# FFN1 of the first two tile pairs: two weight blocks side by side instead of two token tiles, and w1's last rows partly copied on chip

## The chip, the cores and the metric

The kernel runs on one NeuronCore of a Trainium2 chip. The metric is the device time of one execution in microseconds. Engines are named as in the profile: PE is TensorE (PEld its weight loads), DVE is VectorE, ACT is ScalarE, POOL is GpSimd, SP is the queue that issues most DMAs.

## The reference

`x` is 2048 tokens of 448 features, all in bf16. A layer norm feeds two branches whose outputs are added to `x`: a linear attention with 16 heads of 28 features, and a feed-forward network with 1792 hidden features.

```python
xn = _layernorm(x, axis=-1)
return x + _A_ref(xn, A_wqkv, A_w_phi, A_wo) + _B_ref(xn, B_w1, B_w2)

def _B_ref(x, w1, w2):
    h = jnp.einsum("bsd,df->bsf", x, w1)     # FFN1: 448 -> 1792
    h = _silu(h)
    return jnp.einsum("bsf,fd->bsd", h, w2)  # FFN2
# _A_ref: q, k, v = x @ wqkv; phi = [softmax(q w_phi), softmax(-q w_phi)] (k alike);
#         o = phi_q (phi_k^T v) / (phi_q . sum phi_k + 1e-6); o @ wo
```

## The kernel before

The 2048 tokens are 16 tiles of 128, and tiles go in pairs 0 to 7. For each pair the layer norm is taken token by token (`ln_stats`, `ln_rstd`, `ln_norm`), and the normalized rows are turned on TensorE and evicted to `xnT` (`ln_tr`), which has features on partitions. 448 features are seven blocks of 64: `xnT[:, 0:3]` has the first 384 features of the pair's first tile, `xnT[:, 4:7]` those of the second, and block 3 has the last 64 features of the first tile in its upper partitions (UP, 0 to 63) and of the second in its lower ones (LO, 64 to 127).

All matmuls use half of the array's rows: two with 64 rows each, one on UP and one on LO, run side by side and write different PSUM banks (`mms`, L443, whose instructions carry L446). In `contract` (L474) the two halves work on the two tiles of a pair with the same weight block. A first pass takes four steps (UP rows for the first tile, LO rows for the second), a second pass the other halves in three; between the passes stands a wait of PE for itself (`syncs`), since both passes add into the same banks. For this the last 64 rows of each weight (block `KF`) must lie in both halves, so `load_tail` (L548) loads them twice.

FFN1 is `ffn1_chunk` (L672): units of 512 columns in two banks, then one silu on ACT over both (1024 elements per partition). With one pair (`npair` 1) a unit has four feature blocks of 128 and the matmuls move 128 columns; with two pairs it has two blocks and they move 256. Pairs 0 and 1 do feature blocks 0 to 7 one pair at a time, in four units, and blocks 8 to 13 together, in three.

The layer norm of pairs 0 and 1 (`ln_pair_sqrt`, L623) takes the square root on ACT (L630) and the reciprocal on DVE; later pairs take a power on POOL (L599). `ln_pair_first` places matmuls on `ident` (`warm`, L528) around the first transposes. ACT changes from its sqrt table to silu after the square roots of pair 1.

The SP queue issues, in program order: x tile 0, w1 columns 0 to 511 (rows 0 to 383), x tiles 2-3, w1 columns 512 to 1023 with its two tails, x tiles 4-5, w1 columns 1024 to 1791 with its two tails, x tiles 6-7. ACT issues x tile 1 and the first two tails. The loads in `paced` (x tiles 8-11, wqk, x tiles 12-15, wv) wait for the layer norms of pairs 1 to 4; those of w2 and wo wait for exponentials of k.

The order on each engine is not written by hand: a planner (`schedule`, `_Prog`) places every operation by program order, priority and assumed durations, under its data dependences and under order-only ones (`odeps`) within an engine. The instructions then wait on semaphores where the planner saw a dependence.

After FFN1 of pairs 2 to 5 come the folding of `w_phi` into wqk, then k, v, q and the attention state with FFN1 of the rest in between, and then for each pair the second FFN layer and the output projection. In that last phase `q_divide` (L915) makes the attention output of a pair: DVE does the division (L926 to L939), and five additions (`oadd`, L961) bring it into `o_sum`, the tile `xn_sb`. They run on POOL, except that for the last pair all but the first run on DVE. `o_transpose` turns the result on PE into a bank that `out_store` (L990, DVE) must have emptied.

Of the kernel before, what the change touches and what calls it, by code (L numbers as in the profile page):

```python
# [8 lines left out]
ACTF = mybir.ActivationFunctionType  # L9
# [323 lines left out]
def bass_parallel_sum__linear_kernel_hedgehog__dense_activation_silu__prompt_kernel(  # L333
# [12 lines left out]
    KF = 3  # L346
# [8 lines left out]
    with es:  # L355
# [82 lines left out]
        def mm(dst, lhsT, rhs, start, stop, name, dur=None):  # L438
            return P.op("pe", dur or d_mm(_cols(rhs)),
                        lambda e: e.matmul(dst, lhsT, rhs, start=start, stop=stop, skip_group_check=True),  # L440
                        reads=[lhsT, rhs], writes=[dst], table=128, name=name)
# [83 lines left out]
        qpad = wqk_sb[:, :, 0, :, 56:64]  # L525
        P.op("pool", d_pool(256, 0.9), lambda e: e.memset(qpad, 0.0), writes=[qpad], name="qpad")
        P.op("pool", d_pool(256, 0.9), lambda e: e.memset(wraw[:, :, 2 * D:], 0.0), writes=[wraw[:, :, 2 * D:]], name="wpad")
        def warm(n, cols=128):  # L528
            rhs = ident[:, None, :].broadcast_to([128, cols // 128, 128])
            dst = banks[3][:, 0:cols].rearrange("p (a c) -> p a c", c=128)  # L530
            for i in range(n):
                mm(dst, ident[:], rhs, True, True, "warm", cols * 0.836)
            return P.ops[-1]

        def load(dst, src, nbytes, name, eng="sp"):
            return P.dma(lambda e: e.dma_start(out=dst, in_=src), nbytes, writes=[dst], name=name, eng=eng)  # L536
# [4 lines left out]
        def load_x(t0, t1, eng="sp"):  # L541
            return load(x_sb[:, t0:t1, :], xt[:, t0:t1, :], (t1 - t0) * 128 * D * 2, f"x{t0}", eng)

        def load_k(dst, src, c0, c1, name, eng="sp", o=0):
            return load(dst[:, 0:KF, c0 - o:c1 - o], src[0:384, c0:c1].rearrange("(k p) f -> p k f", p=128),
                        384 * (c1 - c0) * 2, name, eng)

        def load_tail(dst, src, c0, c1, name, eng="sp", eng2="sp", o=0):  # L548
            return [load(dst[r, KF, c0 - o:c1 - o], src[384:448, c0:c1], 64 * (c1 - c0) * 2, name, e)
                    for r, e in ((UP, eng), (LO, eng2))]  # L550

        x1_op = load_x(1, 2, "act")
        pre_op.odeps.add(x1_op.id)
        w1t = load_tail(w1_sb, B_w1, 0, 512, "w1at", "act", "act")
        for o in w1t:
            o.odeps.add(pre_op.id)
        load_x(0, 1)
        load_k(w1_sb, B_w1, 0, 512, "w1a")
        load_x(2, 4)
        for c0, c1 in ((512, 1024), (1024, FF)):  # L560
            load_k(w1_sb, B_w1, c0, c1, "w1b")
            load_tail(w1_sb, B_w1, c0, c1, "w1bt")
            if c0 == 512:
                load_x(4, 6)
        load_x(6, 8)
        first_loads = len(P.ops)
        paced = []
# [52 lines left out]
            else:  # L620
                copy_dve(dst, src, "xnT_ev", d_dve(128 * n, 2))

        def ln_pair_sqrt(p):  # L623

            for t in (2 * p, 2 * p + 1):
                k = len(P.ops)
                ln_stats(t)
                if t % 2:
                    P.ops[k].odeps.add(k - 2)
                P.op("act", 220, lambda e, t=t: e.activation(std[:, t:t + 1], mv[:, t, 1:2], ACTF.Sqrt, bias=epsc[:]),  # L630
                     reads=[mv[:, t, 1:2], epsc[:]], writes=[std[:, t:t + 1]], table="sqrt", name="std")
            for t in (2 * p, 2 * p + 1):
                P.op("dve", 150, lambda e, t=t: e.reciprocal(rstd[:, t:t + 1], std[:, t:t + 1]),
                     reads=[std[:, t:t + 1]], writes=[rstd[:, t:t + 1]], name="rstd")
                ln_norm(p, t)

        def ln_pair_first(bk):
            ln_pair_sqrt(0)
            prev = None
            for n, js, eng in ((19, [0, 1, 2], "act"), (2, [3, 4, 5, 6], "dve")):  # L640
                k = len(P.ops)
                o = warm(n, 256)
                if prev:
                    P.ops[k].odeps.add(prev)
                k = len(P.ops)
                ln_tr(0, js, bk if eng == "act" else bk - 2, eng)
                P.ops[k].odeps.add(o.id)
                prev = P.ops[-1].id - 1
            ev = P.ops[-1]
            k = len(P.ops)  # L650
            o = warm(5, 256)
            P.ops[k].odeps.add(prev)
            return ev, o

        def ln_pair(p, one_by_one=False):
            t0, t1 = 2 * p, 2 * p + 1
            for t in (t0, t1):
                ln_stats(t)
                if one_by_one:
                    ln_rstd(t, t + 1)  # L660
            if not one_by_one:
                ln_rstd(t0, t1 + 1)
            ln_norm(p, t0)
            ln_norm(p, t1)
            ln_tr(p, [0, 1, 2, 3, 4, 5, 6], 6, "dve")

        silus = []
        exps = set()
# [3 lines left out]
        def ffn1_chunk(p0, npair, f0, fend, units=(0, 2, 4)):  # L672
            n = npair * 128
            F = 512 // n
            while f0 < fend:
                f1 = min(fend, f0 + F)
                b0 = units[unit_no[0] % len(units)]
                unit_no[0] += 1
                jobs = []
                for ft in range(f0, f1):  # L680
                    jobs.append((lambda r, b: xnT[r, b, p0:p0 + npair, :].rearrange("p a c -> p (a c)"),
                                 lambda r, k, ft=ft: w1_sb[r, k, ft * 128:ft * 128 + 128],
                                 [banks[b0 + par][:, (ft - f0) * n:(ft - f0) * n + n] for par in range(2)],
                                 ft == f0, True))
                units_done.append(contract(jobs, n, True, True, "ffn1_mm"))
                w = f1 - f0
                src = psum[:, b0 * 512:(b0 + 2) * 512].rearrange("p (r c) -> p r c", r=2)[:, :, 0:w * n]
                if w == 1:
                    dst = hT[:, f0, :, p0:p0 + npair, :].rearrange("p r a c -> p r (a c)")
                else:  # L690
                    src = src.rearrange("p r (f c) -> p r f c", f=w)
                    dst = hT[:, f0:f1, :, p0:p0 + npair, :].rearrange("p f r a c -> p r f (a c)")
                o = act(dst, src, ACTF.Silu, "silu", table="silu")
                if exps:
                    o.odeps.update(exps)
                silus.append(o)
                f0 = f1

        def exp_act(dst, src, scale, name):
            o = act(dst, src, ACTF.Exp, name, table="exp", scale=scale)  # L700
# [38 lines left out]
                else:  # L739
                    copy_dve(dst, src, "fold_ev", d_dve(n))  # L740

        last0, warm0 = ln_pair_first(6)
        k = len(P.ops)
        ln_pair_sqrt(1)
        ln_tr(1, [0, 1, 2], 6, "act")
        ln_tr(1, [3, 4, 5, 6], 4, "dve")
        sqrt_last = [o.id for o in P.ops if o.name == "std"][-1]
        for o in P.ops[k:]:
            if o.eng == "dve":
                o.odeps.add(last0.id)  # L750
        last1 = P.ops[-1].id
        k = len(P.ops)
        ffn1_chunk(0, 1, 0, 4, (0, 2))
        P.ops[k].odeps.add(warm0.id)
        silus[0].odeps.add(sqrt_last)
        ffn1_chunk(0, 1, 4, 8, (0, 2))
        ffn1_chunk(1, 1, 0, 4, (4,))
        ffn1_chunk(1, 1, 4, 8, (0,))
        k = len(P.ops)
        ln_pair(2)  # L760
        for o in P.ops[k:]:
            if o.eng == "dve":
                o.odeps.add(last1)
        ln_pair(3)
        ffn1_chunk(0, 2, 8, FT, (2, 4, 0))
        ln_pair(4)
        ffn1_chunk(2, 2, 0, 4)
        ln_pair(5)
        for i in range(3):
            ffn1_chunk(2, 2, 4 + 2 * i, 6 + 2 * i)  # L770
            fold_tr(3 * i)
        ffn1_chunk(2, 2, 10, FT)
        P.cur_prio = 2
        late_constants()
        P.cur_prio = 0
        for kt in range(4):
            ffn1_chunk(4, 2, 2 * kt, 2 + 2 * kt)
            fold(kt)
        ln_pair(6)
        ffn1_chunk(4, 2, 8, 12, (0, 4))  # L780
        ln_pair(7)

# [132 lines left out]
        def q_divide(p):  # L915
# [40 lines left out]
            segs = [seg(0, 0, 0, 448), seg(1, 448, 384, 392), seg(1, 456, 392, 448), seg(1, 512, 0, 336), seg(1, 848, 336, 384)]  # L956
            oadd_last[p] = []
            for i, (dst, a0, a1) in enumerate(segs):
                eng = "dve" if i and p == NPAIR - 1 else "pool"
                o = P.op(eng, d_pool(_cols(dst), 2.26) if eng == "pool" else d_dve(_cols(dst)),  # L960
                         lambda e, dst=dst, a0=a0, a1=a1: e.tensor_tensor(dst, a0, a1, ALU.add),  # L961
                         reads=[a0, a1], writes=[dst], name="oadd")
                oadd_last[p].append(o.id)
# [89 lines left out]
        for a, c in zip(chain, chain[1:]):  # L1053
            for o in c:
                o.odeps.add(a[-1].id)
        evs = [o.id for o in P.ops if o.name == "xnT_ev"]
        for o, d in zip(paced, evs[3:7]):
            o.deps.add(d)
        eks = [o.id for o in P.ops if o.name == "exp_k"]
        for o, d in zip(w2_loads + [wo_load], eks[0::2]):  # L1060
            o.deps.add(d)
# [111 lines left out]
```

## Time and profile before

| | |
|---|---|
| time, median of 3 executions | 158.67 us (158.19 to 159.33) |
| the profiled execution, its own time | 159.27 us |
| its span, first to last instruction | 157.5 us |
| PE busy | 151.2 us (96%), 2655 matmuls |
| DVE, ACT, POOL busy | 100.9, 75.1, 52.9 us |
| granted TensorE clock | 1.0 |
| FFN1 of all pairs (`psum<-xnT,w_sb`) | 896 matmuls, 48.9 us |

A row of the profile gives the line of the kernel, the engine, the operation, the output and inputs by name, and how often it ran; then its busy time, the mean of one, and the idle time before it with what ended it. A row of the timeline begins with the start and the length in microseconds, and in brackets has the idle time before it and its releaser; equal neighbours are merged (x38). The chain of waits is followed back from the last instruction; "issue" in it is time in which the engine waited for nothing that the profile shows. A matmul's end is modelled, so neighbours overlap in the rows.

### The profile page before, as it was taken

The page shows a single profiled execution, that of the slowest core. Times are in us where ns is not written, and L with a number is a line of the kernel's source. Part 1 is how long each engine was busy: PE and PEld are TensorE (multiplying, and loading weights), DVE is VectorE, ACT ScalarE, POOL GpSimd, SP SyncE. Part 2 cuts the span into 40 slices and gives each one's busy share as a digit, 9 for nine tenths or more (in the row PEclk, how much of TensorE's full clock was granted, in tenths as well). Part 3 has the DMA queues.
Part 4 walks back from the last instruction along what each step waited for, and adds up shares of the span by engine and source line. Part 5 has one row for each costly group of instructions (what it writes and reads, how often), then busy time and mean ns, then how long its engine had stood idle before and what let it go on. Part 6 is the DMA issues. An engine that isn't in the chain of part 4 may idle for free.

```text
span 157.5 us, 5805 instructions
## 1 busy us (share of the span) xinstructions
PE 151.2 (96%) x2655; PEld 100.0 (64%) x2655; DVE 100.9 (64%) x180; ACT 75.1 (48%) x88; POOL 52.9 (34%) x74
## 2 busy tenths in 40 slices
PE   6996999999999999999999999999999999999992
PEld 4685888888864445445468887545555655554782
DVE  1886796863236889496796487794755748396203
ACT  3376557458789886996869755120210202022000
POOL 7001111120100777839577023633516060602000
PEclk9999999999999999999999999999999999999999
DMA  4983367000004332040000000001011010101012
GB/s 144 303 262 116 69 163 220 7 0 4 4 0 116 110 113 78 0 121 0 0 4 2 4 4 0 4 4 58 19 43 58 4 58 4 62 2 58 4 58 62
DMA packets 8309, 9.24 MB, mean 59 GB/s; under 512 B 1436, under 2 KB 8028, under 8 KB 8284
## 3 DMA queue, kind: packets, MB, share of 16 engines
q1 hardware_dynamic: 7980, 8.62, 18.2%
q8 instruction: 21, 0.34, 0.9%
q10 hardware_dynamic: 304, 0.25, 0.5%
q14 instruction: 4, 0.03, 0.1%
HBM read 7.02 MB, written 1.84 MB: 56 GB/s over the span
## 4 chain that ended last, share of the span: by engine, by line
PE 88%; DVE 4%; DMA 3%; issue 2%; SPq 2%; DVEq 0%
PE psum L446 85%; DMA w_sb<-in_B_w_dram 3%; PE psum L459 3%; SPq L536 2%; DVE wraw L939 1%; DVE out_sb L990 1%; DVE xn_sb L961 0%; DVE R L926 0%; DVE rden L933 0%; DVE Gq L934 0%; DVE Dd L928 0%; PE psum L877 0%; DVE den L930 0%; DVEq L1113 0%
## 5 line engine op out<-in xcount | busy, mean ns | idle before, releaser
L446 PE MATMUL psum<-xnT,w_sb 64*128 64x256 bf16 (+1 forms) x896 | 48.9, 256 | 1.7 <-issue 1.3
L446 PE MATMUL psum<-w_sb,hT 64*128 64x448 bf16 (+2 forms) x504 | 46.6, 328 | 0.0
L446 PEld LDWEIGHTS psum<-xnT,w_sb 64*128 64x128 bf16 x896 | 37.2, 94 | 7.4 <-issue 1.5
L465 ACT ACTIVATE hT<-psum 128x1024 bf16<-128x1024 f32 x28 | 28.1, 1023 | 15.7 <-PE psum L446 14.3
L446 PEld LDWEIGHTS psum<-w_sb,hT 64*128 64x128 bf16 x504 | 23.1, 94 | 16.1 <-ACT oT L465 0.4
L961 POOL TENSOR_TENSOR xn_sb<-wraw 128x448 bf16<-128x448 f32 (+4 forms) x36 | 19.7, 580 | 36.9 <-DVE wraw L939 36.9
L465 ACT ACTIVATE oT<-psum 128x896 bf16<-128x896 bf16 x8 | 7.3, 917 | 40.8 <-PE psum L459 40.8
L810 POOL TENSOR_TENSOR scr<-scr,Rk 128x1792 bf16<-128x1792 bf16 x6 | 19.3, 3211 | 17.6 <-ACT scr L465 12.7
L465 ACT ACTIVATE EqT<-psum 128x1024 bf16<-128x1024 f32 x16 | 15.5, 1021 | 6.0 <-PE psum L446 6.0
L939 DVE TENSOR_TENSOR wraw<-psum,Gq 128x1792 f32<-128x1792 f32 (+1 forms) x9 | 16.4, 1817 | 0.7
L446 PE MATMUL psum<-xnT,wqk_sb 64*128 64x512 bf16 x112 | 14.8, 378 | 0.0
L990 DVE TENSOR_TENSOR out_sb<-psum,x_sb 128x896 bf16<-128x896 f32 (+2 forms) x9 | 8.8, 980 | 8.6 <-PE psum L446 8.5
L926 DVE RECIPROCAL R<-psum 128x64 f32<-128x64 f32 (+1 forms) x9 | 4.6, 512 | 15.0 <-PE psum L446 15.0
L446 PE MATMUL psum<-wv_sb,xnT 64*128 64x448 bf16 x112 | 14.0, 349 | 0.0
L446 PE MATMUL psum<-wo_sb,oT 64*128 64x448 bf16 (+2 forms) x126 | 13.6, 328 | 0.0
L446 PE MATMUL psum<-wqk_sb,xnT 64*128 64x448 bf16 x112 | 13.2, 349 | 0.0
L590 DVE BATCH_NORM_STATS2 st<-x_sb 128x6 f32<-128x448 bf16 x16 | 9.8, 613 | 4.0 <-DMA x_sb<-in_A_x_dram 4.0
L599 POOL TENSOR_TENSOR rstd<-ve,neghalf 128x2 f32<-128x2 f32 x6 | 4.2, 694 | 24.3 <-DVE ve L598 24.3
L802 DVE TENSOR_REDUCE Sk<-scr 128x64 f32<-128x1792 bf16 x6 | 12.1, 2010 | 0.0
L469 DVE CAST scr<-psum 128x896 bf16<-128x896 f32 x6 | 6.5, 1083 | 8.5 <-PE psum L446 8.5
L465 ACT ACTIVATE scr<-psum 128x896 bf16<-128x896 f32 x12 | 10.4, 915 | 0.7
L446 PEld LDWEIGHTS psum<-wo_sb,oT 64*128 64x128 bf16 x126 | 6.1, 94 | 4.6 <-ACT oT L465 0.2
(64 smaller groups left out, 135.4 us busy)
## 6 DMA issues: line engine op xcount, KB each, us to landing
out_dram<-out_sb SPq DMA_DIRECT2D x7, 224.0 KB, 1.9
w_sb<-in_B_w_dram SPq DMA_DIRECT2D x3, 448.0 KB, 3.4
x_sb<-in_A_x_dram SPq DMA_DIRECT2D x2, 448.0 KB, 4.6
w_sb<-in_B_w_dram SPq DMA_DIRECT2D x2, 384.0 KB, 4.8
x_sb<-in_A_x_dram SPq DMA_DIRECT2D x3, 224.0 KB, 4.9
wraw<-in_A_wqkv_dram SPq DMA_DIRECT2D x1, 672.0 KB, 4.3
w_sb<-in_B_w_dram SPq DMA_DIRECT2D x1, 576.0 KB, 6.6
wv_sb<-in_A_wqkv_dram SPq DMA_DIRECT2D x1, 336.0 KB, 4.8
```

The costliest lines, as they stand in the source:

```text
L446: r = e.matmul(dst, lhsT, rhs, start=start, stop=stop, skip_group_check=True)
L459: out = e.transpose(dst, src, ident[r, 64:128] if r == LO else ident[r, 0:64])
L465: return P.op("act", d_act(_cols(src)), lambda e: e.activation(dst, src, func, scale=scale), reads=[src], writes=[dst], table=table, name= ...
L469: return P.op("dve", dur, lambda e: e.tensor_copy(dst, src), reads=[src], writes=[dst], name=name)
L590: P.op("dve", 600, lambda e: e.bn_stats(st6[:, t, :], x_sb[:, t, :]), reads=[x_sb[:, t, :]], writes=[st6[:, t, :]], name="bnst")
L599: P.op("pool", 580, lambda e: e.tensor_tensor(r2, v2, nh, ALU.pow), reads=[v2, nh], writes=[r2], name="rstd")
L802: P.op("dve", d_dve(896 * n), lambda e, S4=S4, E4=E4: e.tensor_reduce(S4, E4, AXL.X, ALU.add), reads=[E4], writes=[S3], name="Sk")
L810: lambda e, E5=E5, R5=R5: e.tensor_tensor(E5, E5, R5, ALU.mult),
L926: P.op("dve", d_rec(32 * n), lambda e, R3=R3, U=U: e.reciprocal(R3, U[:, :, :, DH + 1]), reads=[U[:, :, :, DH + 1]], writes=[r2], name="R2")
L939: P.op("dve", d_dve(896 * n), lambda e, dsto=dsto, U=U, G3=G3, n=n: e.tensor_tensor(dsto, U[:, :, :, 0:DH], G3[:, :, :, None].broadcast_to ...
L961: lambda e, dst=dst, a0=a0, a1=a1: e.tensor_tensor(dst, a0, a1, ALU.add),
L990: P.op("dve", d_dve(2 * (c1 - c0)), lambda e: e.tensor_tensor(dst, ob, xs, ALU.add), reads=[ob, xs], writes=[dst], name="out_ev")
```

## The change

FFN1 of pairs 0 and 1 gets a function of its own, `ffn1_single`. The two row halves now hold two different weight blocks, and both move the same 256 columns, the two tiles of one pair; the halves change places in the second pass. The last 64 features of both tiles must therefore lie in both halves: the layer norm writes them twice (`lnz_norm`), and they go through PE into a separate tile `xnTt`. The normalized rows and `xnTt` lie in a part of `EqT` that is unused until later. The first unit of a pair does its first pass tile by tile, with 128 columns. Each pair has four units (blocks 0-3, 4-7, 8-11, 12-13).

Evictions of the transposes go by tile: for pair 0 tile 0 on ACT and tile 1 on DVE, for pair 1 tile 2 on DVE and tile 3 on ACT. Pair 1 takes its power on POOL, tile by tile, in place of the square root. The matmuls on `ident` go in row halves. Later users of block 3 of `xnT` for these pairs are served by four DMA copies (`lnz_rest`).

On the SP queue w1's columns 512 to 1023 now stand ahead of x tiles 2-3, and columns 1024 to 1791 ahead of x tiles 4-5. The tails of columns 512 to 1791 are loaded once, into LO, and ACT copies them into UP. The loads in `paced` wait for the last evictions of pairs 1 to 4. Two smaller edits: units of pairs 2 and 3 take the banks in the order 4, 0, 2, and of the last pair's five additions only one (336 columns) stays on DVE.

```diff
-        load_x(2, 4)
-        for c0, c1 in ((512, 1024), (1024, FF)):
-            load_k(w1_sb, B_w1, c0, c1, "w1b")
-            load_tail(w1_sb, B_w1, c0, c1, "w1bt")
-            if c0 == 512:
-                load_x(4, 6)
+        load_k(w1_sb, B_w1, 512, 1024, "w1b")
+        load(w1_sb[LO, KF, 512:FF], B_w1[384:448, 512:FF], 64 * (FF - 512) * 2, "w1t")
+        load_x(2, 4)
+        load_k(w1_sb, B_w1, 1024, FF, "w1c")
+        load_x(4, 6)
         load_x(6, 8)
...
+        def lnz_rest(p):
+            for t, r in enumerate((UP, LO)):
+                a, b = xnT[r, 3, p, :], xnTt[r, p, t, :]
+                o = P.dma(lambda e, a=a, b=b: e.dma_start(out=a, in_=b), 64 * 256, reads=[b], writes=[a], name="xnTt")
...
+            order = [warm(19), lnz_tr(0, 0), warm(3), lnz_tr(0, 1), warm(1)]
+            lnz_ev(0, 0, ("act", "act"))
+            ev = lnz_ev(0, 1, ("dve", "dve"))
...
+        def lnz_second(p):
+            k = len(P.ops)
+            for t in range(2):
+                ln_stats(2 * p + t)
+                ln_rstd(2 * p + t, 2 * p + t + 1)
+            for t in range(2):
+                lnz_norm(p, t)
+                lnz_tr(p, t)
+                ev = lnz_ev(p, t, (("dve", "dve"), ("act", "act"))[t])
...
+        def ffn1_single(p, f0, f1, b0, by_tile=False):
+            h = (f1 - f0) // 2
...
+            for q, t0, t1 in (((0, 0, 1), (0, 1, 2), (1, 0, 2)) if by_tile else ((0, 0, 2), (1, 0, 2))):
+                rr = (UP, LO) if q == 0 else (LO, UP)
+                for k in range(KF + 1 - q):
+                    for i in range(h):
+                        parts = []
+                        for j in range(2):
+                            r, ft = rr[j], f0 + j * h + i
+                            xx = xnTt[r, p, t0:t1, :] if k == KF else xnT[r, k + 4 * t0:k + 4 * t1 - 3:4, p, :]
...
+        a, b = w1_sb[UP, KF, 512:FF], w1_sb[LO, KF, 512:FF]
+        act(a, b, ACTF.Identity, "w1t")
...
+        banks_ = iter((0, 2, 4, 0, 2, 4, 0, 2))
+        for p in range(2):
+            for f0 in range(0, FT, 4):
...
+                done = ffn1_single(p, f0, min(FT, f0 + 4), next(banks_), f0 == 0)
...
-                eng = "dve" if i and p == NPAIR - 1 else "pool"
+                eng = "dve" if i == 3 and p == NPAIR - 1 else "pool"
...
-        for o, d in zip(paced, evs[3:7]):
-            o.deps.add(d)
+        for o, d in zip(paced, evp):
+            o.deps.add(d.id)
```

## The prediction

> **What bounds the kernel now.** I read the page's totals and chain first, then the chain in order of time, then the timeline of each engine where the chain leaves TensorE.
>
> ```profile
> PE 151.2 (96%) x2655; PEld 100.0 (64%) x2655; DVE 100.9 (64%) x180; ACT 75.1 (48%) x88; POOL 52.9 (34%) x74
> q8 instruction: 21, 0.34, 0.9%
> PE 88%; DVE 4%; DMA 3%; issue 2%; SPq 2%; DVEq 0%
> ```
>
> TensorE is busy for 96% and carries 88% of the chain. A change pays only if it gives TensorE less work, an earlier start, or fewer waits. The chain of waits from the start shows where it waits:
>
> ```profile
> 3.52 4.87 DMA w_sb<-in_B_w_dram
> 13.00 1.31 issue
> 14.31 1.21 PE psum L446 x35
> ```
>
> ```profile
> 7.06 1.28 PE L446 MATMUL psum<-xnT,w_sb 64*128 64x128 bf16 x38
> 8.52 0.73 PE L446 MATMUL psum<-xnT,w_sb 64*128 64x128 bf16 x20 [0.18 <-DMA w_sb<-in_B_w_dram]
> 15.49 0.84 PE L446 MATMUL psum<-xnT,w_sb 64*128 64x128 bf16 x24
> 16.17 0.28 PE L459 MATMUL psum<-ident,xn_sb 64*128 64x64 bf16 x8
> 16.29 2.59 PE L446 MATMUL psum<-xnT,w_sb 64*128 64x256 bf16 x44
> 18.71 0.25 PE L459 MATMUL psum<-ident,xn_sb 64*128 64x64 bf16 x6
> ```
>
> This is TensorE's timeline. A matmul of one row half runs beside that of the other, so I count pairs: 12 pairs of 128 columns take 16.17-15.49 = 0.68, **57 ns** each; 22 pairs of 256 columns take 18.71-16.29 = 2.42, **110 ns** each. A 128-column matmul is drawn 216 ns long (the group's mean), so a gap in the chain understates the wait by 216-57 = 0.16 us. FFN1's waits before are then: 0.34 for w1 at 8.4, 0.21 twice where a second pass waits for its first (10.36 and 12.16), 1.31+0.16 = 1.47 at 13.00, and some 0.1 later: **2.3 us**. What ends the 1.47 is no semaphore: the last matmul of the third unit has none. It is TensorE's matmul 222 (26 warm, 28 transposes, 168 FFN1), its instruction 444 with weight loads. The instruction queue's 21 packets serve 5310 instructions, 253 each, and the trace has the first of them only at 11.85 us, while w1 and x still load. I read the wait as an instruction block that came late.
>
> ```profile
> 9.94 1.28 ACT L465 ACT_TABLE_LOAD   x1
> 12.32 0.71 POOL L599 TENSOR_TENSOR rstd<-ve,neghalf 128x2 f32<-128x2 f32 x1 [8.47 <-DVE ve L598]
> 12.47 0.63 DVE L590 BATCH_NORM_STATS2 st<-x_sb 128x6 f32<-128x448 bf16 x1 [0.23 <-DMA x_sb<-in_A_x_dram]
> ```
>
> From these I take prices, and from two of the rows landing times: w1's second tail (1472 KB issued by then) lands at 3.52+4.87 = 8.38, x6-8 (2688 KB) at 12.44: 300 KB/us between.
>
> ```profile
> 141.34 1.79 DVE L961 TENSOR_TENSOR xn_sb<-wraw 128x8 bf16<-128x8 f32 x4
> 141.39 1.13 POOL L961 TENSOR_TENSOR xn_sb<-wraw 128x448 bf16<-128x448 f32 x1 [4.54 <-DVE wraw L939]
> 143.05 1.08 DVE L990 TENSOR_TENSOR out_sb<-psum,x_sb 128x896 bf16<-128x896 f32 x1
> 144.28 0.38 PE L459 MATMUL psum<-ident,xn_sb 64*128 64x64 bf16 x14 [0.22 <-DVE out_sb L990]
> ```
>
> Near the end TensorE waits once more: VectorE does four of the last pair's adds (L961) before the output add (L990) whose bank the last transposes need.
>
> **The change, part by part.**
>
> *TensorE's work.* Before: 112 pairs of 128 and 42 of 256, 6.4+4.6 = 11.0 us. After, by the built order: 32 of 128 and 82 of 256, 1.8+9.0 = 10.8. The two new transpose pairs cost 0.06. **Gain 0.1**: the wider moving operand buys almost nothing, since 128 columns already run at half the price of 256.
>
> *Start.* FFN1 began at 7.06, when VectorE had evicted tile 1. The by-tile unit needs tile 0 alone, evicted by ScalarE in 5.85 to 6.34; with 0.09 to hand over it starts at 6.43. **Gain 0.63**. Tile 1 is evicted by about 7.0, when tile 0's eight pairs are just through (6.9). The dropped w1 tails (320 KB) against one of 160 KB are in the landing times below. Warm matmuls go in halves, the same columns.
>
> *New waits.* I walk the built order. On SP x2-4 moves behind w1b and w1t, x4-6 behind w1c. Landings at 300 KB/us around the 8.38 row: w1t (1280 KB) 7.74, x2-4 (now 1504 KB, behind w1b and w1t) 8.49, w1c (2080 KB) 10.4.
> - The first unit and the second up to its tail rows are 16 pairs of 128 and 12 of 256: 2.2 us, to 8.66. The tail of the upper half waits for ScalarE's copy: 1280 elements, between 0.92 us for 896 and 1.02 for 1024 elements continued, 1.23: 7.79 to 9.02. Wait 0.43.
> - 2 pairs, a pass wait of 0.22, 3 pairs: 9.86. Then tile 2's transposes stand in line. Its input lands at 8.49; stats 0.62, aggregate 0.18, ve 0.17 and hand-overs make 9.58, GpSimd's rstd 0.70 makes 10.35, the normalize 0.37 ends at 10.76. Wait 0.97.
> - At 11.3 a unit needs bank 0, so silu 0: 9.02 + table 1.28 + silu 1.02 = 11.3. No wait, but no slack. w1c is there.
> - Tile 3's normalize (second rstd on GpSimd): 0.2. A pass wait 0.22. Tile 3's eviction behind silu 1 on ScalarE: 0.17. Later some 0.1.
>
> Together **2.3, as much as before**: the 1.47 and the w1 wait go, and waits for the copy, tile 2 and tile 3 take their place. The 1.47 goes because matmul 222 now lies at the end of the unit on bank 4, near 14.5 to 15.3, while the block before it is passed near 7.5, not 9: 7 us for a fetch that took 5.3.
>
> [...]
>
> *x8-12* is issued after tile 3's last eviction, 13.4, where before it was issued by 10.9. The page's 448 KB row lands after 4.6: 18.0, and tile 8's stats, wanted at 17.0, would hold TensorE 0.6. The 112 KB row (2.6) plus 336 KB at 300 gives 3.7 and no wait. The queue is idle then: I take 0.2.
>
> *Nothing on the path:* the four tail copies in lnz_rest stand on SP behind wv and ahead of w2, near 25 to 28 us, where SP waits for the first exponentials until 48.27; uncovered they are four issues of some 0.5. The other bank order and GpSimd's two narrow rstd fall on idle time, apart from those counted.
>
> *The tail.* VectorE keeps one add of four (0.50 for 336 columns), so the output add starts near 141.85, ends at 142.9. GpSimd's four adds end 1.80 after 141.39, or 0.45 later if VectorE's add holds it up: 143.2 to 143.6. TensorE is ready at about 143.8. **Gain 0.4** (0.22 plus the 349-94 ns by which a 448-column matmul is drawn too long, less the usual turn).
>
> ```profile
> L961 DVE TENSOR_TENSOR xn_sb<-wraw 128x56 bf16<-128x56 f32 x1 | 1.2, 1165 | 0.0
> L961 POOL TENSOR_TENSOR xn_sb<-wraw 128x56 bf16<-128x56 f32 x7 | 2.1, 302 | 0.0
> ```
>
> VectorE's 56 columns took 1165 ns while GpSimd's 448-column add ran. [...]
>
> **Sum.** 0.63 + 0.1 + 0.0 - 0.2 + 0.4 = **0.9 us** less. The profiled execution took 159.27 (span 157.5 and 1.77 around it), 0.6 over the median of 158.67, so 158.4 by its own time and **157.8** against the median. From the bounds (x8-12 0 to 0.6, tail 0 to 0.5, landings 0.3 either way) its own range is 157.2 to 158.6.
>
> **Rivals.**
> 1. *The loads come earlier than by the straight line.* If w1t lands at 7.0 and x2-4 at 7.6 (before, x2-4 was third and its stats ran at 6.89), the copy costs nothing, silu 0 ends at 10.6 and the unit at 11.3 starts at 10.4, held by w1c: 0.9 less, **156.9**. For it: w1's 160 KB are gone. Against: 300 KB/us was sustained, and the queue is as full.
> 2. *Slower: ScalarE's queue hangs on the w1 copy.* Behind it stand the table load, silus 0 and 1 and tile 3's eviction. From a landing of about 8.1 each us later costs one; the gain is gone at 9.0, and 10.8 gives 157.8+2.7 = **160.5**. For it: the page's 96 KB tails took 6.2 us to land. Against: those stood behind 576 KB.
> 3. *The 1.47 wait stays*, at its place in the stream or another: **159.3**. For it: no release is recorded. Against: the longer time to fetch.
>
> **How the numbers follow.** Forecast 0.42, rival 1 0.31, rival 2 0.14, rival 3 0.13. A measurement of this kernel tells about 1% from no change: faster than 157.08 is rival 1, 0.31; slower than 160.26 is rival 2, 0.14; the rest 0.55. The range, 156.5 to 159.7, takes in rivals 1 and 3 and leaves out most of rival 2.
>
> **What would show it.** First FFN1 matmul near 6.4; a 1.2 us copy on ScalarE ending near 9.0; TensorE idle near 9.9 for about 1 us with VectorE's normalize as releaser; no "issue" wait near 13 to 15; no wait for out_sb before the last transposes. An idle stretch of over 1.5 us before 20 us, or a first silu after 11, would make the prediction wrong.

## The result: 0.9% slower, and the profile after

The changed kernel takes 159.6 us (median of 18 executions, 158.81 to 161.48), the kernel before 158.18 us beside it (18 executions, 157.84 to 159.33). The ratio is 1.0089, interval 1.0068 to 1.011: a loss of some 1.4 us where 0.9 us less had been forecast.

The first view is the page of the changed kernel's profiled execution (its own time 161.48, span 159.7): totals, granted clock over the 40 slices, the instruction queue, the chain by engine.

```profile
PE 152.8 (96%) x2599; PEld 99.3 (62%) x2599; DVE 100.1 (63%) x181; ACT 76.1 (48%) x90; POOL 55.0 (34%) x79
...
PEclk9996999999999999999999999999999999999999
...
q8 instruction: 20, 0.33, 0.8%
...
PE 87%; ACT 5%; DMA 4%; issue 1%; SPq 1%; DVE 0%; ACTq 0%
```

Two things are new. ScalarE, absent from the chain before, holds 5% of it. And the clock line has a 6 in its fourth slice: this execution ran 3.41 us at half clock, which most do not (14 of the 18 have a mean clock of 0.998 or more), so sizes below are read from another execution of the same kernel (span 157.3, clock 1.0; "the changed kernel, again"). The chain in order of time shows ScalarE's first part, in the same execution as the page:

```profile
2.23 7.04 DMA w_sb<-in_B_w_dram
9.27 0.02 issue
9.30 1.27 ACT w_sb L465
10.56 0.02 issue
10.58 1.28 ACT L465
11.86 0.01 issue
11.88 1.03 ACT hT L465
```

Read it as one line of dominoes: the w1 tail lands at 9.27, ScalarE copies it, loads the silu table, does silu 0, and only then may TensorE use bank 0 again at 12.96.

For the changed kernel, again, TensorE's timeline in the first FFN1 units (start, length, work, idle time before and its releaser):

```profile
6.47 0.50 PE L446 MATMUL psum<-xnT,w_sb 64*128 64x128 bf16 x12
7.90 0.29 PE L446 MATMUL psum<-EqT,w_sb 64*128 64x128 bf16 x4 [0.94 <-issue]
...
9.80 0.38 PE L446 MATMUL psum<-EqT,w_sb 64*128 64x256 bf16 x4
10.25 0.50 PE L446 MATMUL psum<-xnT,w_sb 64*128 64x256 bf16 x6
10.90 0.26 PE L459 MATMUL psum<-ident,EqT 64*128 64x64 bf16 x6
...
11.88 0.39 PE L446 MATMUL psum<-xnT,w_sb 64*128 64x256 bf16 x4 [0.33 <-ACT hT L465]
```

FFN1 starts at 6.47, but its fourth step, the one that needs w1's first tails, stands until 7.90. The profile names no releaser; the transfers in the trace show the second of the first tails landing at 7.81. Counted as the prediction counted, from start to start less the pitch of the pair ahead (57 or 110 ns), FFN1's waits are 1.10 for the first tails, 0.23 for a second pass, 0.31 for tile 2, 0.49 for silu 0, 0.23 for a second pass, 0.19 ahead of 13.65 and 0.23 for a second pass at 20.62: **2.8 us**.

Later a second place appears. ScalarE, then TensorE, of the changed kernel, again:

```profile
44.79 1.02 ACT L465 ACTIVATE hT<-psum 128x1024 bf16<-128x1024 f32 x1 [0.34 <-PE psum L459]
47.06 1.28 ACT L465 ACT_TABLE_LOAD   x1 [1.25 <-PE psum L446]
48.36 1.73 ACT L465 ACTIVATE scr<-psum 128x896 bf16<-128x896 f32 x2
49.97 1.95 ACT L465 ACTIVATE EqT<-psum 128x1024 bf16<-128x1024 f32 x2
```

```profile
51.02 0.54 PE L446 MATMUL psum<-wv_sb,xnT 64*128 64x448 bf16 x4
51.97 1.04 PE L446 MATMUL psum<-xnT,wqk_sb 64*128 64x512 bf16 x8 [0.41 <-ACT EqT L465]
```

And the kernel before, run again beside it:

```profile
43.68 1.02 ACT L465 ACTIVATE hT<-psum 128x1024 bf16<-128x1024 f32 x1 [0.55 <-PE psum L459]
44.73 1.28 ACT L465 ACT_TABLE_LOAD   x1
46.02 1.73 ACT L465 ACTIVATE scr<-psum 128x896 bf16<-128x896 f32 x2
```

Before, the exp table is loaded straight behind the last silu, while TensorE works on k. After, the load stands idle 1.25 us for TensorE's semaphore, its 1.28 us fall on the path, and TensorE waits for a bank at 51.97.

The tail, VectorE, GpSimd and TensorE of the changed kernel, again:

```profile
141.65 0.51 DVE L1039 TENSOR_TENSOR xn_sb<-wraw 128x336 bf16<-128x336 f32 x1
142.08 1.08 DVE L1068 TENSOR_TENSOR out_sb<-psum,x_sb 128x896 bf16<-128x896 f32 x1
```

```profile
141.79 2.03 POOL L1039 TENSOR_TENSOR xn_sb<-wraw 128x448 bf16<-128x448 f32 x4 [4.56 <-DVE wraw L1017]
```

```profile
143.52 0.92 PE L446 MATMUL psum<-wo_sb,oT 64*128 64x448 bf16 x8
144.27 0.37 PE L459 MATMUL psum<-ident,xn_sb 64*128 64x64 bf16 x14
```

The output add starts 0.43 after the one add left on VectorE instead of 1.71, and TensorE goes on without waiting for out_sb.

To see where the time went I cut each span at four starts: first FFN1 matmul, first k matmul, the transposes of the kv state, last group of the output projection. All in us.

| kernel | FFN1 starts | to k | k to kv | kv to end | end |
|---|---|---|---|---|---|
| before (execution of the prediction) | 7.06 | 37.87 | 43.04 | 66.27 | 154.24 |
| before, again | 7.57 | 36.05 | 43.05 | 66.26 | 152.93 |
| changed, again | 6.47 | 38.26 | 43.63 | 65.91 | 154.27 |
| changed minus before, both again | -1.10 | +2.21 | +0.58 | -0.35 | +1.34 |

There is a gain at the start and a gain at the end; the stretch from FFN1 to k and the exp table give back more than both. About half of the 1.10 at the start is chance, as the next section shows.

### The profile page after: what moved, and what is told of

Its sections match the earlier page's. It is cut to its first block, busy times and chain, and to the rows that moved or that the text cites. A ratio compares the mean times of both kernels' runs of the same rounds, so it can differ in the third digit from the quotient of the medians.

```text
span 159.7 us, 5705 instructions
## 1 busy us (share of the span) xinstructions
PE 152.8 (96%) x2599; PEld 99.3 (62%) x2599; DVE 100.1 (63%) x181; ACT 76.1 (48%) x90; POOL 55.0 (34%) x79
## 4 chain that ended last, share of the span: by engine, by line
PE 87%; ACT 5%; DMA 4%; issue 1%; SPq 1%; DVE 0%; ACTq 0%
PE psum L446 84%; DMA w_sb<-in_B_w_dram 4%; PE psum L459 3%; ACT L465 2%; ACT EqT L465 1%; SPq L538 1%; ACT w_sb L465 1%; ACT hT L465 1%; ACT scr L465 1%; DVE out_sb L1068 0%; PE psum L955 0%; ACTq L1190 0%
## 5 line engine op out<-in xcount | busy, mean ns | idle before, releaser
L446 PE MATMUL psum<-xnT,w_sb 64*128 64x256 bf16 (+1 forms) x780 | 49.6, 271 | 1.0 <-DMA w_sb<-in_B_w_dram 0.4
L446 PEld LDWEIGHTS psum<-xnT,w_sb 64*128 64x128 bf16 x780 | 35.3, 96 | 7.7 <-PE psum L446 1.7
L465 ACT ACTIVATE hT<-psum 128x1024 bf16<-128x1024 f32 (+1 forms) x29 | 28.4, 995 | 15.4 <-PE psum L446 15.0
L1039 POOL TENSOR_TENSOR xn_sb<-wraw 128x448 bf16<-128x448 f32 (+4 forms) x39 | 20.6, 560 | 36.9 <-DVE wraw L1017 36.9
L465 ACT ACTIVATE EqT<-psum 128x1024 bf16<-128x1024 f32 (+1 forms) x18 | 16.1, 940 | 5.6 <-PE psum L446 5.6
L603 POOL TENSOR_TENSOR rstd<-ve,neghalf 128x2 f32<-128x2 f32 (+1 forms) x8 | 5.4, 670 | 25.9 <-DVE ve L602 25.9
L446 PEld LDWEIGHTS psum<-xnT,wqk_sb 64*128 64x128 bf16 x112 | 4.7, 94 | 6.9 <-PE psum L446 1.7
```

Of the source, the lines that this page charges most:

```text
L446: r = e.matmul(dst, lhsT, rhs, start=start, stop=stop, skip_group_check=True)
L465: return P.op("act", d_act(_cols(src)), lambda e: e.activation(dst, src, func, scale=scale), reads=[src], writes=[dst], table=table, name= ...
L603: P.op("pool", 580, lambda e: e.tensor_tensor(r2, v2, nh, ALU.pow), reads=[v2, nh], writes=[r2], name="rstd")
```

## The experiments

Ratios are to the kernel before, run beside each on the same chip, with 95% intervals. One percent is 1.58 us. "Swap" below is the edit of the third experiment. Times of single stretches come from one profiled execution each.

### The two kernels again, unchanged

> The kernel before, once more. Theory W (a wait that is usually not there): the 1.47 us wait of TensorE at 13.00 in the first profile is not typical; here matmul 222 follows its neighbour without a pause, FFN1 of pairs 0 and 1 ends about 1.3 us earlier and the span is near 156.4. Rival (the wait belongs to the kernel): the wait of over 1 us before matmul 222 is there again, and the span is near 157.5.

Measured: 0.9993 (0.9964 to 1.0022). The 1.47 us wait of the prediction does not come back: at the same matmul 222 there is no gap in this execution, nor in the two later kernels with the old FFN1. It was an accident of one execution, worth most of the difference in span, 157.5 against 156.0. TensorE's row runs through:

```profile
10.12 4.11 PE L446 MATMUL psum<-xnT,w_sb 64*128 64x128 bf16 x122
14.06 0.25 PE L459 MATMUL psum<-ident,xn_sb 64*128 64x64 bf16 x6
```

The packets of the instruction queue in the traces speak for a block that came late in that one execution. There the first packet starts at 11.85, when 196 matmuls had started, and matmul 222 follows its end by 1.38 us. In the execution again it starts at 10.51, after 142 matmuls, and in the twelve others after 118 to 156. Why it was late there is not known.

A second accident lies at the start. The traces' records of the clock at full begin at another moment in each execution: at 5.36 us in the execution of the prediction and 5.42 in the changed kernel, again, but at 7.14 in this one. The two matmuls on `ident` behind the first transposes show it, in the execution of the prediction and in this one:

```profile
5.72 0.39 PE L440 MATMUL psum<-ident 128*128 128x256 bf16 x2
5.86 0.60 PE L440 MATMUL psum<-ident 128*128 128x256 bf16 x2
```

So FFN1 begins late here (7.57 against 7.06), and by that difference I put some 0.5 of the 1.10 in the table down to the clock. The page's clock line shows nothing of it: it reads 9 there in every execution.

> The changed kernel, once more. Theory P (three parts): even without a halved clock it is 1.2 to 1.6 us slower than before, made of TensorE's waits before 20 us (about +1.2 against a run before without its long wait), the exp table load that ScalarE begins only after the k product (about +0.6 near 50 us), and the tail (-0.35). First k matmul near 45.0, transposes of the attention state near 88.8 us. Rival C (the clock): the excess comes from a clock window at half rate; with the clock at 1.0 throughout the span would be near 156.5 to 157.

Measured: 1.0062 (1.0037 to 1.0086), slower in a second comparison too. The half clock is not there, so it is no cause of the loss; the profile of it was shown above.

### The order of two waits (swap)

The first exponential of k waits for two semaphores. In the rows above the table load comes behind the one that the program states first: in the kernel before that is VectorE's, long given, and the load starts 0.03 us behind the last silu; in the changed kernel it is TensorE's, and the load stands idle 1.25 us for it. Which is first follows from the iteration order of a set.

```diff
+                first = o.eng == "act" and o.name == "exp_k" and ("dma", -1) not in waited
+                if first:
+                    waited[("dma", -1)] = 1
+                    need = dict(sorted(need.items(), key=lambda kv: kv[0] != ("eng", "pe")))
                 for key, (sm, val) in need.items():
```

> The changed kernel with one edit: the first exponential of k waits for the same two semaphores in the other order. Theory T: the table load then stands behind VectorE's semaphore, long given, and not behind TensorE's; it runs before the k product ends, the first exponential follows the product at once, TensorE's wait for EqT near 54 us goes, and the time falls by 0.5 to 0.7 us (ratio to before near 1.005). Rival: the table load costs ScalarE only slack; TensorE's order absorbs it and the time stays within 0.15 us of the changed kernel (ratio 1.009).

Measured: 1.0044 (1.0016 to 1.0072); k to kv is 43.05 again, and the table load stands 0.02 us behind the last silu. The mechanism is shown by the stretch; the intervals of 1.0062 and 1.0044 overlap too much to size it. It is tried again further down.

### The tail edit alone

In the kernel before:

```diff
-                eng = "dve" if i and p == NPAIR - 1 else "pool"
+                eng = "dve" if i == 3 and p == NPAIR - 1 else "pool"
```

> The kernel before with the tail edit alone (one of the last pair's five additions on VectorE in place of four). Theory: 0.35 to 0.4 us faster (ratio 0.9977), the transposes of the last pair follow the output projection with no wait for out_sb, and VectorE's 336-column add takes about 0.5 us because it starts ahead of GpSimd's. [...]

Measured: 0.9962 (0.994 to 0.9984), a gain by itself. Kv to end is 65.93 against 66.26: 0.33 us, the whole of the step in the table. The ratio would be 0.6 us, with an interval that holds 0.33.

### The old order of x and w1, the tails loaded twice, and both

All three start from the changed kernel with the swap. The comments in the excerpt below are not in the code; they say which of the three runs has the line.

```diff
+        load_x(2, 4)                                   # first and third
         load_k(w1_sb, B_w1, 512, 1024, "w1b")
-        load(w1_sb[LO, KF, 512:FF], ..., "w1t")        # second and third
+        load_tail(w1_sb, B_w1, 512, FF, "w1t")
-        load_x(2, 4)                                   # first and third
...
-        act(a, b, ACTF.Identity, "w1t")                # second and third
```

> The changed kernel with the waits of e_wait and one more edit: x tiles 2-3 are loaded again ahead of w1's columns 512 to 1023 and the single tail. Theory S (ScalarE's chain decides: tail landing, copy 1.27, table load 1.28, silu 0): tile 2's layer norm comes some 1.5 us earlier, but the tail lands 0.5 to 0.9 later, the copy ends near 10, silu 0 near 12.5, and TensorE waits there instead: first k matmul at 44.8 to 45.3, time within 0.3 us of e_wait. Rival X (tile 2's layer norm decides): first k matmul near 44.2 and 0.5 us faster than e_wait.

Measured: 1.0039 (1.0012 to 1.0066), no different from 1.0044. TensorE's timeline:

```profile
7.80 0.29 PE L446 MATMUL psum<-EqT,w_sb 64*128 64x128 bf16 x4 [0.31 <-issue]
...
9.10 1.48 PE L446 MATMUL psum<-xnT,w_sb 64*128 64x256 bf16 x24 [0.57 <-DMA w_sb<-in_B_w_dram]
11.46 0.40 PE L446 MATMUL psum<-EqT,w_sb 64*128 64x256 bf16 x4 [0.87 <-ACT w_sb L465]
...
13.70 0.76 PE L446 MATMUL psum<-xnT,w_sb 64*128 64x256 bf16 x6 [0.76 <-ACT hT L465]
```

Tile 2 is in time, there is no wait for its transposes any more. But w1's columns and tail now stand behind x tiles 2-3; the tail lands at 10.02 against 8.88, and the columns (0.57), the copy (0.87) and silu 0 behind it (0.76) hold TensorE instead. In this execution the clock falls to half at 13.81, behind these waits.

> The changed kernel with the waits of e_wait and no copy on ScalarE: the tails of columns 512 to 1791 are loaded twice (2 x 160 KB) where the change loads them once. Theory S: the table load follows tile 0's evictions at once and ends near 8, silu 0 ends near 10.5; but x tiles 2-3 land 0.4 to 0.5 later, so tile 2's layer norm takes over as the wait: first k matmul 44.3 to 44.9, time 0 to 0.4 us less than e_wait. Rival (the copy alone is the cost): 0.8 us or more less than e_wait, TensorE without a wait of over 0.5 us from 8 to 13.

Measured: 1.005 (1.0024 to 1.0076), again nothing. No copy stands on ScalarE, but the second tail is 160 KB more ahead of x tiles 2-3, which land at 9.93 against 9.28 with the swap alone. They are late, and so are the first tails:

```profile
8.28 0.29 PE L446 MATMUL psum<-EqT,w_sb 64*128 64x128 bf16 x4 [1.25 <-issue]
...
12.28 0.43 PE L459 MATMUL psum<-ident,EqT 64*128 64x64 bf16 x8 [0.24 <-DVE EqT L633]
```

> Both edits at once, on the changed kernel with the waits of e_wait: x tiles 2-3 ahead of w1b, and the tails loaded twice with no copy. Theory S and X together (two waits side by side, either hides what the other's removal brings): first k matmul near 43.8 to 44.1, 0.7 to 1.0 us less than e_wait, about 0.3 under the kernel before (ratio 0.998). Rival (the new FFN1 itself costs, by its first unit that needs w1's first tail sooner): no more than 0.3 us less than e_wait.

Measured: **0.9968** (0.9948 to 0.9989), faster than both kernels. The two edits that did nothing alone gain 0.76%, 1.2 us, together:

```profile
6.81 0.56 PE L446 MATMUL psum<-xnT,w_sb 64*128 64x128 bf16 x12
7.21 0.27 PE L446 MATMUL psum<-EqT,w_sb 64*128 64x128 bf16 x4
...
8.10 1.48 PE L446 MATMUL psum<-xnT,w_sb 64*128 64x256 bf16 x24 [0.17 <-DMA w_sb<-in_B_w_dram]
9.42 0.38 PE L446 MATMUL psum<-EqT,w_sb 64*128 64x256 bf16 x4
```

The waits for the tails, the copy and tile 2 are all gone; FFN1 to k takes 36.89 us against 38.68 with the swap alone. (Two later kernels with the same loads and the same FFN1 take 37.45 and 37.07, so part of this is chance.) The two edits need each other. Each alone sets one load ahead and the other back. Together, tile 2's layer norm is in time, and without the copy the tails may land as late as 8.60 and 9.21, since TensorE wants them at 9.42. How much of the 1.2 us belongs to the first tails, which land at 6.43 here and at 7.96 with the swap alone, is not told apart.

### The new order of loads alone, in the kernel before

`load_x(2, 4)` goes behind w1b and its tails, `load_x(4, 6)` behind w1c and its tails; nothing else.

> The kernel before with the load order alone changed: w1's columns 512 to 1023 with both tails ahead of x tiles 2-3, columns 1024 to 1791 with both tails ahead of x tiles 4-5. Theory L (the order of the loads costs by itself): tiles 2-3 land near 8.4 to 9 in place of 6.5, pair 1's layer norm holds TensorE 0.5 to 1.0 us near 10, and the time rises by 0.4 to 0.9 us (ratio 1.003 to 1.006). Rival: the old FFN1 has pair 0's blocks 4 to 7 to do meanwhile and the order costs nothing (ratio 1.000).

Measured: 1.0039 (1.0021 to 1.0056), slower by 0.6 us. VectorE, then TensorE:

```profile
8.48 0.63 DVE L588 BATCH_NORM_STATS2 st<-x_sb 128x6 f32<-128x448 bf16 x1 [1.64 <-DMA x_sb<-in_A_x_dram]
```

```profile
10.39 0.26 PE L459 MATMUL psum<-ident,xn_sb 64*128 64x64 bf16 x6 [1.35 <-DVE xn_sb L604]
```

The old FFN1 pays for late x tiles in the same way. What is shown here is that this order of loads costs by itself with the old form of FFN1. With the new form the old order of x alone gained nothing (1.0039 against 1.0044).

### The new FFN1 alone

The kernel with both edits (the swap is in it too), and the four adds of the last pair back on VectorE.

```diff
-                eng = "dve" if i == 3 and p == NPAIR - 1 else "pool"
+                eng = "dve" if i and p == NPAIR - 1 else "pool"
```

> The kernel with x tiles 2-3 first and the tails loaded twice (0.9968 of the kernel before, with the last pair's adds on GpSimd), but with the last pair's four adds back on VectorE as before: what is left is the new FFN1 of pairs 0 and 1 alone, under the old order of loads. Theory A (the new FFN1 itself is worth nothing, the adds were the whole gain of 0.35 us): ratio 0.999 to 1.001, the stretch from the first kv transpose to the end back at 66.4 us. Theory B (the new FFN1 gains by its earlier start once its loads are in time, up to the 0.6 us of the prediction): ratio 0.995 to 0.997. Theory C (the new FFN1 costs something and the adds gain more than 0.35): 1.002 or more.

Measured: 0.9981 (0.9961 to 1.0002), between theories A and B. The interval holds no gain as well as one of 0.6 us, and excludes a loss that matters. Kv to end is 66.18: the adds give 0.26 of it here.

### The swap undone where nothing else waits

The kernel with both edits, without the swap; no engine's order differs otherwise.

> The kernel with x tiles 2-3 first and the tails loaded twice (0.9968), with the two waits of the first exponential of k back in the order of the changed kernel, so that the exp table load stands behind the semaphore of TensorE. Nothing else differs in any engine's order. Theory A (the load of 1.28 us is exposed and TensorE waits for it): the stretch from the first k matmul to the first kv transpose goes from 43.04 to 43.6 us, the time rises by 0.5 to 0.6 us, ratio 1.000 to 1.001. Theory B (the wait is made good before the end, as the comparison of the changed kernel with and without it, 0.4 us apart, would let one think in part): stretch 43.6 but time up by 0.3 or less, ratio under 0.999.

Measured: 1.0001 (0.998 to 1.0023) against 0.9968 (0.9948 to 0.9989): 0.33% or 0.5 us, as the first theory said, though the intervals just meet and leave the size open. K to kv is 43.62 against 43.04, and that 0.58 is the firmer figure. ScalarE:

```profile
43.71 1.02 ACT L465 ACTIVATE hT<-psum 128x1024 bf16<-128x1024 f32 x1 [0.33 <-PE psum L459]
45.98 1.28 ACT L465 ACT_TABLE_LOAD   x1 [1.25 <-PE psum L446]
```

The row is the same as in the changed kernel, 1.25 of idle ahead of the load included.

### The first lower tail on SP

```diff
-        w1t = load_tail(w1_sb, B_w1, 0, 512, "w1at", "act", "act")
...
+        w1t = load(w1_sb[UP, KF, 0:512], ..., "w1at", "act")
...
         load_x(0, 1)
+        load(w1_sb[LO, KF, 0:512], ..., "w1at")
```

> The changed kernel with the two waits of the first exponential in the old order (1.0044), and the first tail of w1 for the lower half issued by SP behind x tile 0 instead of by ScalarE as its third load. The planner moves a few of pair 1's and 2's transposes by it; the work is the same. Theory A (the wait of about 1 us at 7 us is for this tail alone, and hides nothing): the tail lands before 6.7, the wait at 7 is gone, but the waits for the copy and for tile 2 behind it grow by most of it, since their transfers are not earlier: gain 0 to 0.4 us, ratio 1.002 to 1.0045. Theory B (the three waits add up): the gain is the whole 1.0 us, ratio 0.998.

Measured: 1.0085 (1.0056 to 1.0114), slower by 0.65 us than without it. Both theories missed. TensorE:

```profile
7.97 0.51 PE L446 MATMUL psum<-xnT,w_sb 64*128 64x128 bf16 x12 [0.96 <-DMA w_sb<-in_B_w_dram]
8.30 0.29 PE L446 MATMUL psum<-EqT,w_sb 64*128 64x128 bf16 x4
...
9.48 1.48 PE L446 MATMUL psum<-xnT,w_sb 64*128 64x256 bf16 x24 [0.45 <-DMA w_sb<-in_B_w_dram]
11.29 0.39 PE L446 MATMUL psum<-EqT,w_sb 64*128 64x256 bf16 x4 [0.32 <-ACT w_sb L465]
...
12.79 0.26 PE L459 MATMUL psum<-ident,EqT 64*128 64x64 bf16 x6 [0.54 <-DVE EqT L633]
```

The wait for the tail is gone at 8.30 and stands ahead of the first matmul, for the w1 columns that were issued behind it: they land at 7.83 against 4.91. One more issue on SP takes 0.53 us there, and all loads behind it come later by that or more: w1's later tail lands at 9.86 against 8.88, x tiles 2-3 at 10.45 against 9.28. Why the first columns lose 2.9 us by an issue of 0.53 is not shown.

> The kernel with x tiles 2-3 first and the tails loaded twice (0.9968), with the same first tail issued by SP behind x tile 0. Nothing else moves on any engine. Theory A (there the tail landed at 6.43, in time, and no wait of over 0.4 us is left before 20 us): no gain, ratio 0.996 to 0.998, and 64 KB ahead of w1a may delay w1a by 0.2 us. Theory B (in most executions the tail comes as late as the 7.2 to 8.2 us of the other kernels, and the one profile was lucky): gain of 0.3 us or more, ratio 0.995 or less.

Measured: 0.9992 (0.9976 to 1.0009): 0.4 us more than without it, with intervals that overlap. Neither theory had it. There was no such wait to take away, so there is no gain; whether the one more issue is paid here is not told from chance, since FFN1 to k, at 37.36, lies within the 36.89 to 37.45 of the three kernels without it.

## Why the prediction was wrong, step by step

**The start** (0.63) was right: with the clock at full from about the same moment, FFN1 begins at 6.47 against 7.06. In all executions but the two with the first tail on SP it begins at 6.47 to 6.98 with the new form and at 6.93 to 7.57 with the old one, latest in each where the clock came up last.

**TensorE's work** (0.1) was right in that it is nothing: 151.0 us busy against 151.2, and the new FFN1 with x tiles 2-3 first is 0 to 0.6 us faster, no more than its earlier start.

**"2.3, as much as before"** is the step that failed, first of all in what it takes away.
- The waits before were 2.3 only in the execution that I read. Of them 1.47 was the gap without a releaser, which I took as a block of instructions that comes late every time. It does not recur. Counted the same way, the execution again has 0.6 (0.22 and 0.23 for the second passes, 0.12 later); the wait for w1 (0.34) is missing too, since FFN1 begins later there. So 1.7 us of the expected exchange does not exist beside that execution. The prediction went on to 157.8 by taking off 0.6 for an execution slower than the median, though the gap of 1.47 alone more than accounts for that 0.6. That the block is late every time, and the 5.3 us for its fetch, was my estimate from that one execution; the three others with the old FFN1 do not show the gap, and no trace shows when a block is asked for.
- The new waits are 2.8 in one execution and 3.1 in that with the swap, against 2.3. That the sum is near is luck, for its parts are others. The wait for the first tails (1.10 and 0.95) was not in the walk: I let them land as before. Tile 2 (0.97) is 0.31 and 0.51, since TensorE comes later. Silu 0, predicted none, is 0.49 and 0.45. The copy (0.43) is nothing and 0.37, and 1.00 in the profiled execution. Only the second passes are as walked (0.22, measured 0.23). Behind the copy and silu 0 stand landings: w1's tail at 8.20, 8.88 and 9.27, not at 7.74.

**The copy** took 1.27 us, predicted 1.23, and the chain copy, table, silu 0 ran as walked. What was off was its beginning. The line of 300 KB/us was early by 0.5 to 1.5 us for w1t and by 0.1 to 1.2 us for x tiles 2-3 (8.56 and 9.64, predicted 8.49).

**What ScalarE does next** was not walked. I put the exp table load nowhere, as it existed before and was hidden. Its place behind one wait or the other follows from the iteration order of a set and came out differently in the two kernels. It cost 0.58 us in the trace and some 0.5 in time.

**x tiles 8-11** (0.2): no gap of TensorE after 14 us answers to them; nothing.

**The tail** (0.4) was right, 0.35. VectorE's one add took 0.51, predicted 0.50; GpSimd's four took 2.03, between 1.80 and 0.45 more. VectorE's time goes with which of the two starts first: in the new FFN1 alone, where the adds are back on VectorE, its 336 columns start 0.08 behind a GpSimd add of 1152 ns and take 1442; in the changed kernel, again, they start 0.14 ahead and take 0.51 us. No run shows the 0 at the low end of the tail's bounds: with one add left VectorE started ahead by 0.05 (the tail edit alone) to 0.14 and took 0.51 us.

So -0.9 becomes +1.34 in the table: 1.7 for old waits that were not there, 0.5 more of new waits, 0.58 for the exp table, and 0.1 and 0.05 that TensorE's work and the tail fell short, less 0.47 of start that this pair of executions gained beyond 0.63, and less the 0.2 for x tiles 8-11. That makes +1.36.

**The rivals.** Rival 2, ScalarE's queue behind the w1 copy, had a part of the mechanism. With w1t landing at 8.20 and 8.88 (swap) the first k matmul comes at 44.73 and 45.41, one for one as its price was; with 9.27 (the profiled execution, less 1.7 that I estimate for 3.41 us at half clock) it is 45.42, no later. But x tiles 2-3 land later by as much in each (8.56, 9.28, 9.64), and the kernel without the copy was no faster, so the copy alone is not the cause. It got a chance of 0.14 because I trusted the landing line. Rival 1, earlier loads, is the opposite of what came. Rival 3 fell with the gap.

Two things stay open. What made the packet ahead of the gap of 1.47 late is not known, only that the gap is no part of the kernel's usual time. And it is not settled why the second of the first tails comes late: it lands at 7.05 to 8.19 where w1b is issued straight behind w1a and at 6.25 to 7.71 where x tiles 2-3 stand between, two ranges that overlap, and in the profiled execution of the changed kernel the wait for it was only 0.17. The order of loads has a part in it, and so has chance.

## What to carry to other kernels

Before a gap without a releaser enters a sum, see it in a second execution. When two preparations share a queue, setting one ahead sets the other back (w1's tail landed at 10.02 instead of 8.88 here), and a wait that is taken away counts only if nothing else stands behind it: here each of two edits was worth nothing and both 1.2 us. And when an edit moves operations of an engine, ask of every table load behind them which semaphore it stands behind (here it stood idle 1.25 us behind one and 0.02 behind the other); that can be changed without a change in any data.

## What the runs showed of the hardware

TensorE's clock fell to half in the middle of the run, with TensorE at work for half of the time before it. The windows view of the profiled execution of the changed kernel, just before the fall and during it (columns: stretch and length, then busy time of PE, PEld, DVE, ACT, POOL, then granted clock, DMA share and GB/s):

```profile
9.80:13.20 3.40, 1.85 (x32) 0.90 (x32) 3.03 (x12) 3.37 (x4) 1.20 (x2) 1.00 0.28 100
13.20:16.70 3.50, 3.44 (x54) 2.60 (x50) 3.36 (x12) 1.76 (x4) 0.70 (x1) 0.51 0.14 16
```

TensorE was busy for 1.85 of 3.40 us and was then granted half the clock for 3.413 us. In the execution without the fall, the changed kernel, again, it was busy for 2.79 in the same stretch. The kernel with the old order of x alone fell likewise, after 1.71 busy of 3.40.

The other traces narrow it down. In the profiled execution of the changed kernel the first record of full clock begins at 6.399 us and the fall 6.826 later, twice 3.413. Thirteen of the fourteen traces have records of the clock, and with stretches of 3.413 us counted off from the first record of full clock, every stretch in which TensorE is drawn busy for 1.87 us or less is followed by half clock (the two above and thirteen at the ends of the runs), and none with 2.06 or more. The emptiest without a fall stands in the kernel before with the new order of loads:

```profile
7.52:10.93 3.41, 2.06 (x66) 1.60 (x60) 2.30 (x9) 0.80 (x3) 0.00 (x0) 1.00 1.01 301
```

By my estimate a fall costs 1.7 us, half of 3.413, where there is work, so waits that add up within one such stretch can cost more than their sum.
